# V for three of eight attention units, fetched as all-head tiles into the weight staging tiles

## The chip, the core and the metric

The kernel runs on one core of a Trainium2 chip. The number that counts is the device time of one execution in microseconds (us). Three runs of the kernel before took 2112.99, 2114.51 and 2115.87 us, so the median is 2114.51 us. The core has five engines that each work through an instruction list of their own: TensorE (PE, with its weight loads as PEld), VectorE (DVE), ScalarE (ACT), GpSimd (POOL) and SyncE (SP). SP issues all of this kernel's transfers between memory and the core.

## What is computed

A banded attention, and then a mixture of experts (MoE) whose routing weights are balanced by Sinkhorn iterations:

```python
scores = q @ k.T / sqrt(64) + bias          # 4 batches, 8 heads, 768 positions, 64 per head
a = softmax(scores where key < 8 or 0 <= pos - key < 96)
x = (a @ v) as (3072, 512)
P = exp(x @ w_gate - max)                   # (3072, 8)
for _ in range(8):
    P /= P.sum(1) + 1e-9; P /= P.sum(0) + 1e-9; P *= 3072 / 8
out = sum_e P[:, e] * (relu(x @ w1[e]) @ w2[e])
```

The expert products are made with fewer multiplications than the plain rule needs: sums and differences of blocks of x (named b11, b21, b22, t1 to t4) meet sums and differences of blocks of w1 (s1 to s4, a11, a12, a22), after Strassen. Each operand is split into a high and a low half, so a product is three matmuls.

## The kernel before, in words

**The attention.** It is worked in 8 units `u` of 384 rows (half a batch, all heads), each in 4 steps, one for a pair of heads. So there are 32 pairs n = 0 to 31, and unit u holds pairs 4u to 4u + 3. The change's "units 4 to 6" are u = 3, 4 and 5. In step n, PE multiplies the weights of pair n - 1 with V (`values`, tile `o_ps`), turns the weights of pair n (`t_ps`), transposes Q and K of pair n + 3 (`prepare`, tile `tp`) and makes the scores of pair n + 2 (`s_ps`). POOL copies parts of the key tile `kk` for the prepared pair (L278 to L285); the scores of that pair, a step later, need them. Between the steps (`between`) PE does pieces of other work: the gate and the first expert slices of finished rows (`filler`).

**V.** A pair's V is loaded by `load_v`, called by `flush` two pairs ahead, into the tile that the pair two before used: even pairs into a part of `acc` (`early_raw`), odd ones into `raw2`. For odd u a pair takes 6 transfers (L211 to L213 for each head), for even u 4 (L209, L230, L231).

**The sums of x.** When 4 tiles of 128 rows are finished, `sums_of` makes t3, t2, t1 and t4 of them (`combine`, from L706). For all but the last half of the last batch a sum is 5 POOL instructions: `xres` (L706, the low parts), `xsum` (L713), high part (L714), `xsum` (L715), low part (L716). The last half is made with `hurry`: only `xres` (L706) on POOL, then on DVE `xsum` (L708) and its sum with `xres` (L709), ACT rounds it (L710) and DVE takes the low part (L711). The four hurried sums follow each other, because t2 needs t3 and t4 needs t2, and because `xres` has one buffer.

**The experts' weights.** `stage_group` loads a slice of w1 and w2 into the staging tiles `w1f` and `w2f`, and POOL makes four sums of w1 in `wsum` (L637, 128x256 each). `make_group` splits all into high and low halves (ACT L619, POOL L620; tiles `w1ops`, `w2ops`, `s2ops`) and makes four sums of w2 in `wsum2` (L637). `stage` has one buffer for each of these tiles. Group 0 is staged by a call at the last unit, `make(0)` follows the attention, and group g + 1 is made while group g is multiplied.

**What sets the order.** The program hands its instructions to a scheduler, which orders each engine's list beforehand by its own estimate of when each can start. On the chip an engine then takes its list in that order. So an instruction that depends on little (staging group 0, for example) stands far ahead of its place in the code, and a change of one dependence moves instructions everywhere. PE's list in the attention is fixed by the code (`InOrder`); POOL's, DVE's, ACT's and SP's are not.

**The switch.** After the attention, PE multiplies group 0 for the last batch (`layer1_fast`): products p1 and p2 into `bank_x`, p6 into `bank_y` (needs t2), p5 and p3 into `bank_z` (p5 needs t1), p7 and p4 into `bank_w` (p4 needs t4). The Sinkhorn iterations (`ngm_ps`, `c_ps` on PE, small DVE instructions) run among them.

Of the kernel before, what the change touches and what calls it, by code (L numbers as in the profile page):

```python
# [8 lines left out]
F32 = mybir.dt.float32  # L9
# [8 lines left out]
P = 128  # L18
BIG = 2.0 ** 100
MAX_LOCAL = 97  # L20
MAX_GLOBAL = 32
SINKHORN_ITERS = 8
EPS = 1e-9
UT = 3
# [8 lines left out]
WARM2 = 2  # L33
AHEAD = 6
CHUNK = 3
LAG = 7
FG = 2
OPS = ("s1", "s2", "s3", "s4", "a11", "a12", "a22")
# [54 lines left out]
class InOrder:  # L93


    def __init__(self, tc):
        self.tc, self.engine = tc, tc.nc.tensor
# [8 lines left out]
class Banded:  # L106
# [6 lines left out]
    def __init__(self, tc, q, k, v, early):  # L113

        self.tc, self.nc = tc, tc.nc
        self.q, self.k, self.v = q, k, v
        self.H, self.D = q.shape[1], q.shape[3]
        H, nb = self.H, 3 * self.H * P
        self.bias1 = early[:, 0:2 * H * P].rearrange("p (h c) -> p h c", h=H)
        self.bias0 = early[:, 2 * H * P:nb].rearrange("p (h c) -> p h c", h=H)  # L120
        self.early_raw = early[:, nb:nb + self.RAW]
        nb += self.RAW
        self.d1 = early[:, nb:nb + 2 * P]
        self.d0 = early[:, nb + 2 * P:nb + 3 * P]
        self.gates = early[:, nb:nb + BU]
        self.work = [(b, half, g) for b in range(q.shape[0]) for half in range(2) for g in range(H // 2)]
        self.pending, self.waiting = [], []
        self.sums, self.inv, self.outs = {}, {}, {}
        self.pe = InOrder(tc)
        nb += 4 * P  # L130
        self.early_pT = [early[:, n:n + 4 * P].rearrange("p (c k) -> p c k", c=4) for n in (nb, nb + 4 * P)]
        assert nb + 8 * P <= early.shape[1]
        self.warm = early[:, -256:].bitcast(mybir.dt.bfloat16)
        self.qk, self.vs, self.ready, self.scored, self.far, self.copied, self.loaded = {}, {}, {}, {}, {}, {}, {}

    def open(self, ctx, ident, idle):
# [105 lines left out]
        self.qk[n] = q_r, k_r  # L242

    def load_v(self, n):
        if n >= len(self.work):
            return
        self.vs[n] = self.raw_tile(n, 2, 2)
        self.load_pair(self.vs[n], self.v, n)

    def prepare(self, t):  # L250

# [114 lines left out]
    def turn(self, t):  # L366
# [4 lines left out]
        for c, (u, a, _, _, _) in enumerate(blocks):  # L371
            self.pe.transpose(out=t_ps[:, c], in_=p_sb[:, u, a], identity=self.ident)
        pT = self.wrk.tile([P, 4, P], F32, name="pT", bufs=1) if t % CHUNK == 0 else self.early_pT[t % CHUNK - 1]
        copy = self.nc.vector.tensor_copy if self.idle and t % CHUNK == CHUNK - 1 else self.nc.scalar.copy
        copy(out=pT[:, 0:len(blocks)], in_=t_ps[:, 0:len(blocks)])
        return pT

    def values(self, n, group, pT, o_ps):

        D, v_r = self.D, self.vs[n]  # L380
        for c, (u, a, j, i, slots) in sorted(enumerate(self.blocks(n, group)), key=lambda b: b[1][1]):
            self.pe.matmul(o_ps[j * D:(j + 1) * D, i], lhsT=v_r[:, slots[a], j * D:(j + 1) * D],
                           rhs=pT[:, c], start=(a == 0), stop=(a == len(slots) - 1))

    def ahead(self, ts, warm=0):
# [6 lines left out]
    def unit(self, u, x, between):  # L392

        NG, per = len(GROUPS), len(GROUPS) * (self.H // 2)
        if u == 0:
# [7 lines left out]
            self.keep_warm(self.po, "o", WARM0)  # L403
            self.ahead(range(0, CHUNK - 1))
            self.scale_bias(2)
# [4 lines left out]
            self.keep_warm(self.po, "o", WARM1)  # L410
            self.ahead(range(CHUNK - 1, CHUNK))
            self.keep_warm(self.po, "o", WARM1)
            for t in range(CHUNK, AHEAD, CHUNK):
                self.ahead(range(t, t + CHUNK), WARM2)
            for t in range(2 * NG, AHEAD + NG):
# [28 lines left out]
    def flush(self):  # L444


        ended = None
        for n, group, pT, o_ps, g, x in self.pending:
            self.values(n, group, pT, o_ps)
            if group == len(GROUPS) - 1:  # L450
                ended = n, o_ps, g, x
        self.pending = []
        if ended is None:
            return
        n, o_ps, g, x = ended
        self.load_v(n + 2)
        self.nc.vector.tensor_tensor(out=o_ps, in0=o_ps, in1=self.inv.pop(n), op=ALU.mult)
        of = o_ps.rearrange("p t c -> p (t c)")
        for xh, xl, src, dst, width in x:
            self.nc.scalar.copy(out=xh[:, g, dst:dst + width], in_=of[:, src:src + width])  # L460
        for xh, xl, src, dst, width in x:
            self.nc.vector.tensor_tensor(out=xl[:, g, dst:dst + width], in0=of[:, src:src + width],
                                         in1=xh[:, g, dst:dst + width], op=ALU.subtract)
# [457 lines left out]
def pipeline(tc, attention, ident, moe, acc):  # L921
# [11 lines left out]
    with ExitStack() as top:  # L933
# [10 lines left out]
        stage = early.enter_context(tc.tile_pool(name="stage", bufs=1))  # L944
# [5 lines left out]
        pieces = att.enter_context(tc.tile_pool(name="pieces", bufs=4))  # L950
        fps = att.enter_context(tc.tile_pool(name="fps", bufs=2, space=PSUM))
        attention.open(att, ident, (fps, "fl"))
        xs, ops = {}, {}
        ws, spills, making = [], [], []

# [94 lines left out]
        slots = attention.SLOTS  # L1050
        bounds = [0]
        while bounds[-1] < TT - HB:
            t = bounds[-1]
            b = t // BT
            last = ((b + 1) * BT if (b + 1) * BT - t <= HB else t + (UT if b == 0 else HB))
            bounds.append(last)
        chunks = [(t // BT, t % BT, n - t) for t, n in zip(bounds, bounds[1:])]
        opens = [((n - 1) // UT + 1) * slots + LAG for n in bounds[1:]]
        closes = opens[1:] + [NU * slots]
# [12 lines left out]
        def between(n=1):  # L1072
            spill(n)
            now[0] += n
            if now[0] > slots and making:
# [3 lines left out]
                making.clear()  # L1079
            while halves and now[0] >= halves[0][0] * slots + LAG:  # L1080
                h = halves.pop(0)[1]
# [6 lines left out]
        for u in range(NU):  # L1088
            if (u + 1) * UT > (NB - 1) * BT and NB - 1 not in xs:
                while halves and halves[0][1] < 2 * (NB - 2):  # L1090
                    h = halves.pop(0)[1]
# [19 lines left out]
        while halves:  # L1111
            h = halves.pop(0)[1]
# [15 lines left out]
        b = NB - 1  # L1128
# [153 lines left out]
        for q, b in enumerate(order):  # L1282
            x_ops, x_next = x_next, {}
            ms = {}
            for g in range(NG):
# [4 lines left out]
                if g < PLAIN:  # L1290
                    h = Fast(moe, pbc[q, e], h32, spool2, hop)
# [78 lines left out]
def kernel(  # L1370
# [33 lines left out]
    with tc.If(rv > 0) as cmp:  # L1404
        pipeline(tc, band, ident, moe, acc)
    with cmp.Else():
        pipeline(tc, Dense(tc, q, k, v, ng, nl), ident, moe, acc)
# [32 lines left out]
```

## Time and profile before

| | us |
|---|---|
| median of 3 runs | 2114.51 |
| the profiled execution: its span, first to last instruction | 2114.1 |
| PE busy | 2089.4 (99%) |
| DVE busy | 1493.1 (71%) |
| POOL busy | 1511.4 (71%) |
| ACT busy | 742.2 (35%) |

The profiled execution has no time of its own beside its span; the median of the runs is 0.4 us longer than that span, well inside the 2.9 us between the fastest and the slowest run. Times in the rows are microseconds from the span's start. The attention lasts until about 261 us, the switch until about 300 us, and the rest is experts' products.

### The profile page before, as it was taken

The numbers are of one execution on the slowest core, as the hardware profiler recorded it, in microseconds if no ns is written. First come the engines' busy times: TensorE is split into PE (matmuls) and PEld (weight loads), VectorE is DVE, ScalarE is ACT, GpSimd is POOL, SyncE is SP. The second block draws the span as 40 slices with busy tenths as digits, with TensorE's granted clock in tenths as the row PEclk, the third lists the DMA queues.
The fourth block names the chain that finished last, engine by engine and source line by source line (L and its number), as shares of the span: only waits on it lengthen the run. The fifth ranks groups of instructions, "written<-read, shape, count | busy, mean of one in ns | idle before, by whom it ended". The sixth has DMA issues, their size and how long they took to land.

```text
span 2114.1 us, 31113 instructions
## 1 busy us (share of the span) xinstructions
PE 2089.4 (99%) x10435; PEld 1726.2 (82%) x10436; DVE 1493.1 (71%) x2280; ACT 742.2 (35%) x1535; POOL 1511.4 (71%) x1353
## 2 busy tenths in 40 slices
PE   8999999999999999999999999999999999999998
PEld 6887878888888888888888888888788888888887
DVE  7676599565555655557777777777667777777776
ACT  7888743332323333242222222222232222222221
POOL 5677897777767777357777777777677777777776
PEclk9999999999999999999999999999999999999999
DMA  6777566666565665697767766776976776667662
GB/s 147 187 203 197 154 248 243 235 230 246 219 251 214 234 239 218 249 379 204 204 194 203 203 196 201 204 203 195 362 221 196 201 204 203 195 204 204 193 194 83
DMA packets 294871, 452.39 MB, mean 214 GB/s; under 512 B 114160, under 2 KB 153264, under 8 KB 284336
## 3 DMA queue, kind: packets, MB, share of 16 engines
q1 hardware_dynamic: 294704, 450.31, 67.4%
q8 instruction: 87, 1.43, 0.3%
q14 instruction: 80, 0.66, 0.1%
HBM read 310.92 MB, written 139.30 MB: 213 GB/s over the span
## 4 chain that ended last, share of the span: by engine, by line
PE 92%; DVE 3%; ACT 2%; DMA 1%; issue 0%; POOL 0%; SPq 0%; ACTq 0%; DVEq 0%
PE m_ps L100 27%; PE y_ps L100 16%; PE bank_w L100 11%; PE bank_z L100 11%; PE bank_x L100 11%; PE bank_y L100 6%; PE o_ps L100 1%; PE t_ps L103 1%; PE s_ps L100 1%; PE h_ps L100 1%; DVE p_sb L338 1%; PE tp L103 1%; ACT p_sb L352 1%; PE y_ps L798 1%; PE y_ps L799 1%; PE y_ps L800 1%
## 5 line engine op out<-in xcount | busy, mean ns | idle before, releaser
L100 PE MATMUL m_ps<-hop,w2r 128*128 128x512 f32 x2520 | 639.5, 389 | 1.6 <-DVE m L1344 1.4
L1344 DVE TENSOR_TENSOR m<-m_ps,m 128x1024 f32<-128x1024 f32 x406 | 495.4, 1221 | 194.4 <-PE m_ps L100 191.2
L100 PEld LDWEIGHTS m_ps<-hop,w2r 128*128 128x128 f32 x2520 | 472.8, 188 | 100.6 <-DVE m L1344 1.8
L896 POOL TENSOR_TENSOR hop<-h,hop 128x512 fp32r<-128x512 f32 x180 | 234.3, 1301 | 302.8 <-ACT hop L895 302.8
L100 PE MATMUL y_ps<-w2ops,hop 128*128 128x512 f32 x1344 | 336.7, 389 | 0.1
L896 POOL TENSOR_TENSOR hop<-hsum,hop 128x512 fp32r<-128x512 f32 x240 | 306.7, 1300 | 0.9 <-ACT hop L895 0.9
L895 ACT CAST hop<-hsum 128x512 fp32r<-128x512 f32 x240 | 149.4, 623 | 427.0 <-POOL hsum L901 422.8
L100 PEld LDWEIGHTS y_ps<-w2ops,hop 128*128 128x128 f32 x1344 | 252.2, 188 | 52.9 <-DVE acc L1188 0.5
L1188 DVE SCALAR_TENSOR_TENSOR acc<-y_ps,pm,acc 128x512 f32<-128x512 f32 x240 | 179.8, 750 | 143.2 <-PE y_ps L100 141.4
L895 ACT CAST hop<-h 128x512 fp32r<-128x512 f32 x180 | 111.9, 621 | 378.6 <-DVE h L907 367.6
L100 PE MATMUL bank_w<-xr,w1r 128*128 128x512 f32 x744 | 189.0, 389 | 0.0
L100 PE MATMUL bank_z<-xr,w1r 128*128 128x512 f32 x744 | 189.0, 389 | 0.0
L100 PE MATMUL bank_x<-xr,w1r 128*128 128x512 f32 x744 | 188.9, 389 | 0.0
L901 POOL TENSOR_TENSOR hsum<-h,h 128x512 f32<-128x512 f32 x120 | 153.1, 1298 | 41.2 <-DVE h L907 41.1
L100 PEld LDWEIGHTS bank_x<-xr,w1r 128*128 128x128 f32 x744 | 139.6, 188 | 29.0
L100 PEld LDWEIGHTS bank_w<-xr,w1r 128*128 128x128 f32 x744 | 139.5, 188 | 28.9
L100 PEld LDWEIGHTS bank_z<-xr,w1r 128*128 128x128 f32 x744 | 139.5, 188 | 28.9
L901 POOL TENSOR_TENSOR hsum<-h,hsum 128x512 f32<-128x512 f32 x120 | 155.8, 1298 | 0.0
L637 POOL TENSOR_TENSOR wsum<-w1f 128x256 f32<-128x256 f32 x62 | 45.4, 753 | 92.7 <-DMA w1f<-in_moe_w_dram 92.5
L352 ACT ACTIVATE p_sb<-p_sb,mx 128x256 f32<-128x256 f32 (+1 forms) x192 | 93.3, 494 | 7.5 <-DVE mx L338 6.8
L100 PE MATMUL bank_y<-xr,w1r 128*128 128x512 f32 x372 | 94.4, 389 | 0.0
L772 DVE TENSOR_TENSOR t<-bank_y,t 128x512 f32<-128x512 f32 x93 | 64.2, 690 | 40.0 <-PE bank_y L100 39.3
(251 smaller groups left out, 3358.6 us busy)
## 6 DMA issues: line engine op xcount, KB each, us to landing
w1r<-w1s SPq DMA_DIRECT2D x434, 256.0 KB, 2.9
w2r<-w2s SPq DMA_DIRECT2D x420, 256.0 KB, 2.9
w1s<-w1ops SPq DMA_DIRECT2D x31, 1792.0 KB, 6.8
w2s<-s2ops SPq DMA_DIRECT2D x30, 1024.0 KB, 8.5
w2s<-w2ops SPq DMA_DIRECT2D x30, 768.0 KB, 7.7
w1f<-in_moe_w_dram SPq DMA_DIRECT2D x32, 512.0 KB, 7.9
w2f<-in_moe_w_dram SPq DMA_DIRECT2D x32, 512.0 KB, 8.4
xs_t<-piece SPq DMA_DIRECT2D x16, 512.0 KB, 3.5
```

What stands on the lines that cost most here:

```text
L100: return self.tc.keep_in_program_order(self.engine.matmul(*args, **kw))
L103: return self.tc.keep_in_program_order(self.engine.transpose(*args, **kw))
L338: nc.vector.tensor_tensor_reduce(out=pv, in0=s_list[u], in1=bias, scale=-(D ** -0.5), scalar=3.0e38, op0=ALU.add, op1=ALU.min, accum_out=m ...
L352: nc.scalar.activation(out=pv, in_=pv, func=AF.Exp, bias=mx[:, u:u + 1], scale=-1.0, accum_out=sm[:, i, j:j + 1])
L637: self.nc.gpsimd.tensor_tensor(out=s[:, n], in0=x, in1=y, op=op)
L772: tt(out=t, in0=bank["y"], in1=t, op=ALU.add)
L798: self.pe.matmul(y_ps, lhsT=hh, rhs=lf, start=(f == 0), stop=False, skip_group_check=True)
L895: self.nc.scalar.copy(out=t[:, 0], in_=full)
L896: self.nc.gpsimd.tensor_tensor(out=t[:, 1], in0=full, in1=t[:, 0], op=ALU.subtract)
L901: self.nc.gpsimd.tensor_tensor(out=t, in0=self.full[x], in1=self.full[y], op=ALU.subtract)
L1188: nc.vector.scalar_tensor_tensor(out=a, in0=y_ps, scalar=moe.pm[:, tt, e:e + 1], in1=a, op0=ALU.mult, op1=ALU.add)
L1344: nc.vector.tensor_tensor(out=ms[p], in0=bank, in1=ms[p], op=ALU.add)
```

## The change

For u = 3, 4 and 5 (`WIDE`) V is loaded for all four pairs at once, as tiles of 128 keys by 8 heads by 64 (512 columns), while the unit before is worked (`load_wide`, called by `flush` for the pair four ahead). `load_v` skips these units. The tiles are the staging tiles: halves of `w1f`, `w2f` and `wsum` for u = 3 and 5, halves of `wsum2` and one half each of `early_raw` and `raw2` for u = 4. `values` takes each block of V from a list in place of one tile. The 64 transfers of V for these units (24, 16 and 24) become 23 (9, 5 and 9) with the same bytes.

```diff
+WIDE = (3, 4, 5)
...
     def load_v(self, n):
-        if n >= len(self.work):
+        if n >= len(self.work) or n // self.pairs in self.wide:
             return
...
+    def wide_tiles(self, u):
+        stage, W = self.stage, self.H * self.D
+        if u % 2:
+            ts = [stage.tile([P, 4, 2 * P], F32, name="w1f"), stage.tile([P, 2, 4 * P], F32, name="w2f"),
+                  stage.tile([P, 4, 2, P], F32, name="wsum")]
+            flat = [t.rearrange("p a c -> p (a c)") for t in ts[0:2]] + [ts[2].rearrange("p a b c -> p (a b c)")]
+            return [t[:, n * W:(n + 1) * W] for t in flat for n in range(2)]
+        pair = stage.tile([P, 4, 2 * P], F32, name="wsum2").rearrange("p a c -> p (a c)")
+        return [pair[:, 0:W], pair[:, W:2 * W], self.early_raw[:, 2 * UT * P:2 * UT * P + W],
+                self.raw.tile([P, 2 * UT * P], F32, name="raw2")[:, 0:W]]
+
+    def load_wide(self, n):
+        u, part = divmod(n, self.pairs)
+        if u not in self.wide or part == self.pairs - 1:
+            return
...
+        ts, G, dma = self.wide[u], MAX_GLOBAL, self.nc.sync.dma_start
+        own = ts[1 + part] if half == 0 else ts[2 * part + 1]
+        dma(out=own, in_=rows[:, half * UT + part])
+        if half == 1:
+            dma(out=ts[2 * part][G:], in_=rows[G:, UT - 1 + part])
+            dma(out=ts[2 * part][0:G], in_=rows[0:G, 0])
+        elif part == 0:
+            dma(out=ts[0][0:G], in_=rows[0:G, 0])
+            dma(out=ts[0][G:], in_=rows[G:, 1])
...
-            self.pe.matmul(o_ps[j * D:(j + 1) * D, i], lhsT=v_r[:, slots[a], j * D:(j + 1) * D],
+            self.pe.matmul(o_ps[j * D:(j + 1) * D, i], lhsT=v_r[slots[a]][:, j * D:(j + 1) * D],
...
         self.load_v(n + 2)
+        self.load_wide(n + self.pairs)
```

Since `w1f`, `w2f` and `wsum` hold V until u = 5 has read it, the staging of expert group 0 comes after that. In POOL's list the eight sums of group 0 move from the third unit to the seventh (u = 6), and this moves what stands behind them. Line numbers of the changed kernel are larger by 39 or 40 from `prepare` on.

POOL's list where u = 6 begins, before (`xsum` and `xres` are the first instructions of a sum of x, `kk` and `far` the key copies of pair 27):

```order
L713 TENSOR_TENSOR xsum<-xh 128x512
L706 TENSOR_TENSOR xres<-xl 128x512
L278 COPY kk<-kk 128x2x32
L279 COPY kk<-kk 128x2x96
L278 COPY far_3672<-kk 128x2x32
L279 COPY far_3672<-kk 128x2x96
L283 COPY kk<-far_3298 128x2x128
```

and of the change, the same place:

```order
L753 TENSOR_TENSOR xsum<-xh 128x512
L677 TENSOR_TENSOR wsum<-w1f 128x256 x2
L746 TENSOR_TENSOR xres<-xl 128x512
L677 TENSOR_TENSOR wsum<-wsum,w1f 128x256
L317 COPY kk<-kk 128x2x32
L318 COPY kk<-kk 128x2x96
L317 COPY far_3633<-kk 128x2x32
L318 COPY far_3633<-kk 128x2x96
L677 TENSOR_TENSOR wsum_4632<-w2f 128x256 x2
L322 COPY kk<-far_3266 128x2x128
```

Three of the sums of w1 of group 0 now stand ahead of the key copies, and the first of them reads `w1f`, which is fetched only when u = 5 has read its V from it.

POOL's list at the switch, before (the `xres` are those of the four hurried sums t3, t2, t1 and t4; the first `w1ops` and `w2ops` are the splits of group 0, the `wsum` are of group 1):

```order
L620 TENSOR_TENSOR w1ops<-w1f,w1ops 128x2x256
L706 TENSOR_TENSOR xres<-xl 128x512
L620 TENSOR_TENSOR w1ops<-wsum,w1ops 128x4x256
L620 TENSOR_TENSOR w1ops<-w1f,w1ops 128x256
L620 TENSOR_TENSOR w2ops<-w2f,w2ops 128x2x256 x2
L706 TENSOR_TENSOR xres<-xl 128x512 x2
L637 TENSOR_TENSOR wsum<-w1f 128x256 x2
L706 TENSOR_TENSOR xres<-xl,xh 128x512
```

and of the change, from the first hurried `xres` to the third (all others are of group 1; `wsum_4796` is `wsum2`):

```order
L746 TENSOR_TENSOR xres<-xl 128x512
L677 TENSOR_TENSOR wsum<-w1f 128x256 x2
L677 TENSOR_TENSOR wsum<-wsum,w1f 128x256
L660 TENSOR_TENSOR w1ops<-w1f,w1ops 128x2x256
L660 TENSOR_TENSOR w1ops<-w1f,w1ops 128x256
L677 TENSOR_TENSOR wsum<-w1f,wsum 128x256
L746 TENSOR_TENSOR xres<-xl 128x512
L677 TENSOR_TENSOR wsum_4796<-w2f 128x256 x2
L660 TENSOR_TENSOR w2ops<-w2f,w2ops 128x2x256 x2
L660 TENSOR_TENSOR w1ops<-wsum,w1ops 128x4x256
L677 TENSOR_TENSOR wsum_4796<-wsum_4796,w2f 128x256
L746 TENSOR_TENSOR xres<-xl 128x512
```

The splits of group 0 now all stand ahead of the first `xres`, 6 instructions of group 1 stand between the first and the second, and 6 more between the second and the third.

PE's list at the same switch, of the change (`y_ps` is the last filler work, `bank_y` needs t2 and `bank_z` needs t1):

```order
L851 MATMUL y_ps<-w2h,fhop 128x512
L890 MATMUL ngm_ps<-gmax,ones 128x1
L901 MATMUL c_ps<-pm,ones 128x192
L770 MATMUL bank_y<-xh,w1ops 128x512
L771 MATMUL bank_y<-xh,w1ops 128x512
L772 MATMUL bank_y<-xh,w1ops 128x512
L770 MATMUL bank_y<-xh,w1ops 128x512
L771 MATMUL bank_y<-xh,w1ops 128x512
L772 MATMUL bank_y<-xh,w1ops 128x512
L901 MATMUL c_ps<-pm,ones 128x192 x2
L770 MATMUL bank_z<-xh,w1ops 128x512
```

Before, the one `ngm_ps` stood between `bank_y` and `bank_z` and the first `c_ps` came later; the matmuls of `y_ps`, `bank_y` and `bank_z` follow each other in the same order in both.

## Rows read from the trace of the kernel before

**Rows 1.** The page: busy time by engine, and the chain that ended last.

```profile
PE 2089.4 (99%) x10435; PEld 1726.2 (82%) x10436; DVE 1493.1 (71%) x2280; ACT 742.2 (35%) x1535; POOL 1511.4 (71%) x1353
...
PE 92%; DVE 3%; ACT 2%; DMA 1%; issue 0%; POOL 0%; SPq 0%; ACTq 0%; DVEq 0%
```

**Rows 2.** Windows (us from:to; length, busy and count by engine, clock, DMA).

```profile
320.00:340.00 20.00, 20.00 (x91) 16.60 (x89) 19.13 (x37) 6.63 (x11) 14.27 (x13) 1.00 0.72 277
```

**Rows 3.** Waits of PE, 0 to 500 us (waiter <- releaser: us in total, times, longest).

```profile
PE o_ps L100 <- DMA raw<-in_v_dram: 2.6, 3, 1.3
...
PE tp L103 <- DMA raw<-in_q_dram: 1.2, 1, 1.2
...
PE o_ps L100 <- DMA acc<-in_v_dram: 0.6, 1, 0.6
```

**Rows 4.** Timeline of PE (start, us, instruction, [idle before <- releaser]).

```profile
158.84 0.43 PE L100 MATMUL o_ps<-pT,raw 128*64 128x128 f32 x2 [1.25 <-DMA raw<-in_v_dram]
...
277.45 0.39 PE L730 MATMUL bank_y<-xh,w1ops 128*128 128x512 f32 x1
...
281.00 0.50 PE L730 MATMUL bank_z<-xh,w1ops 128*128 128x512 f32 x1 [1.71 <-DVE xh L711]
```

**Rows 5.** Instructions on V's tensor: ns min/median/max, first and last start.

```profile
L211 SPq DMA_DIRECT2D acc<-in_v_dram x16: 382/418/907, 39.1 to 235.5; - x16
```

**Rows 6.** Timeline of POOL, u = 6 to the switch.

```profile
230.20 0.50 POOL L285 CAST kk<-kk 128x384 fp32r<-128x384 f32 x1 [1.72 <-DVE kk L270]
...
235.88 1.27 POOL L714 TENSOR_TENSOR xl<-xsum,xres 128x512 fp32r<-128x512 f32 x1
...
242.46 2.37 POOL L620 TENSOR_TENSOR s2ops<-wsum,s2ops 128x1024 fp32r<-128x1024 f32 x1
...
257.94 1.28 POOL L714 TENSOR_TENSOR xl<-xsum,xres 128x512 fp32r<-128x512 f32 x1
...
262.11 1.75 POOL L620 TENSOR_TENSOR w1ops<-w1f,w1ops 128x512 fp32r<-128x512 f32 x1 [0.16 <-ACT w1ops L619]
...
271.50 1.28 POOL L706 TENSOR_TENSOR xres<-xl 128x512 f32<-128x512 f32 x1
274.73 1.29 POOL L706 TENSOR_TENSOR xres<-xl 128x512 f32<-128x512 f32 x1 [1.95 <-DVE xsum L709]
276.92 2.25 POOL L637 TENSOR_TENSOR wsum<-w1f 128x256 f32<-128x256 f32 x2 [0.89 <-DMA w1f<-in_moe_w_dram]
...
281.50 2.97 POOL L620 TENSOR_TENSOR w1ops<-w1f,w1ops 128x512 fp32r<-128x512 f32 x2
284.43 0.73 POOL L637 TENSOR_TENSOR wsum<-w1f,wsum 128x256 f32<-128x256 f32 x1
285.12 2.05 POOL L637 TENSOR_TENSOR wsum<-w2f 128x256 f32<-128x256 f32 x2
287.14 2.55 POOL L620 TENSOR_TENSOR w2ops<-w2f,w2ops 128x512 fp32r<-128x512 f32 x2
```

**Rows 7.** Timeline of ACT, u = 7.

```profile
240.40 1.05 ACT L619 CAST s2ops<-wsum 128x1024 fp32r<-128x1024 f32 x1
...
242.35 0.56 ACT L826 COPY acc<-g_ps 16x512 f32<-16x512 f32 x1
```

**Rows 8.** Timeline of DVE at the switch.

```profile
265.14 2.87 DVE L709 TENSOR_TENSOR xsum<-xsum,xres 128x512 f32<-128x512 f32 x1 [2.44 <-POOL xres L706]
...
277.89 0.67 DVE L709 TENSOR_TENSOR xsum<-xsum,xres 128x512 f32<-128x512 f32 x1
...
279.70 1.25 DVE L711 TENSOR_TENSOR xh<-xsum,xh 128x512 fp32r<-128x512 f32 x1
```

**Rows 9.** Instructions on w1f: its transfers from issue to landing.

```profile
DMA to landing us min/median/max: 3.5/7.9/9.2
```

**Rows 10.** Windows at the end of the span (columns as Rows 2).

```profile
2108.00:2110.00 2.00, 0.35 (x4) 0.11 (x2) 1.40 (x2) 0.00 (x0) 0.00 (x0) 1.00 0.38 140
2110.00:2112.00 2.00, 0.00 (x0) 0.00 (x0) 0.00 (x0) 0.00 (x0) 0.00 (x0) 0.58 0.40 146
```

More of the change, by code (lines that the diff above doesn't have):

```diff
@@ L133, in __init__ @@
         self.warm = early[:, -256:].bitcast(mybir.dt.bfloat16)
+        self.pairs = self.H // 2
+        self.wide = dict.fromkeys(WIDE)
         self.qk, self.vs, self.ready, self.scored, self.far, self.copied, self.loaded = {}, {}, {}, {}, {}, {}, {}
@@ L244, in load_v @@
     def load_v(self, n):
-        if n >= len(self.work):
+        if n >= len(self.work) or n // self.pairs in self.wide:
             return
-        self.vs[n] = self.raw_tile(n, 2, 2)
-        self.load_pair(self.vs[n], self.v, n)
+        t = self.raw_tile(n, 2, 2)
+        self.load_pair(t, self.v, n)
+        self.vs[n] = [t[:, s] for s in range(2 * UT)]
+    def wide_tiles(self, u):
[12 more added lines that the diff above has]
+            return
+        b, half, _ = self.work[n]
+        rows = self.v[b].rearrange("h (t p) d -> p t h d", p=P)
+        if part == 0:
+            ts = self.wide_tiles(u)
+            for m in range(self.pairs):
+                cols = slice(m * P, (m + 1) * P)
+                self.vs[u * self.pairs + m] = [t[:, cols] for t in ts]
+            self.wide[u] = [t.rearrange("p (h d) -> p h d", d=self.D) for t in ts]
+        ts, G, dma = self.wide[u], MAX_GLOBAL, self.nc.sync.dma_start
[7 more added lines that the diff above has]
+            dma(out=ts[0][G:], in_=rows[G:, 1])
     def prepare(self, t):
@@ L952, in pipeline @@
         attention.open(att, ident, (fps, "fl"))
+        attention.stage = stage
         xs, ops = {}, {}
```

## The prediction

> **What bounds the kernel now.** I read the page first, then the windows, PE's waits, and the timelines of PE, POOL and DVE around the places that the change touches.
>
> PE is busy for 2089.4 of 2114.1 us and stands for 92% of the chain that ended last [rows 1]. After the switch it never idles: in 320 to 340 us it is busy 20.00 of 20 us at a granted clock of 1.00 [rows 2]. So a delay of PE before 300 us shifts everything behind it and is never won back, and a stall removed there is won in full. Two places matter: what PE waits for in the attention, and when it gets through the switch.
>
> In the attention the waits for loads are 2.6 us on V in `raw` (three times, the longest 1.3 us; the one at 158.84 stands in the rows), 0.6 us on V in `acc` and 1.2 us on Q [rows 3, 4]. All lie in u = 4 and 5, which are among the changed units.
>
> At the switch PE has one real wait: `bank_z` at 281.00 waits 1.71 us for the DVE instruction that writes t1 [rows 4]. Behind it stands a chain of POOL: the last key copy of the attention at 230.20, then sums and splits with hardly a pause until the `xres` of t1 at 274.73 [rows 6]. It takes 50.8 us from 230.20 to 281.00. The change alters POOL's list here.
>
> **The change, part by part.**
>
> *Waits on loads.* With V there a unit ahead, the V waits go: 2.6 + 0.6 = 3.2 us. The wait on Q goes too if fewer transfers stand before Q's on SP: 1.2 us. I take the whole, g = 4.4 us; the least is 0, if the other loads become late in their turn.
>
> *Transfers.* They become 41 fewer, which costs nothing. But the first of u = 3 are now issued at about 13 us, between loads that the start needs. Six of them at 0.418 us of SP each [rows 5] are 2.5 us. The start has other work in DVE and ACT that covers this; I take 0, at most 1 us without that cover.
>
> *Staging of group 0 in u = 6.* The eight sums of w1, 0.73 us each (at 284.43) [rows 6], are 5.8 us of POOL, and three of them now stand ahead of the key copies of pair 27. POOL has pauses there, so I take 0; a rival below has the other end. What these sums displace, though, comes later: behind the copy of pair 31 POOL now has 8 instructions of sums of x, where 4 stood between that copy and 235.88.
>
> *The switch.* I add up POOL's new list, with the durations of the old one, from the key copy of pair 31, whose time PE sets. It comes g earlier: 230.20 − 4.4 = 225.8.
>
> - the copy, 0.5: 226.3
> - 8 instructions of sums at 1.3 (the one at 235.88) [rows 6]: 236.7. Before, 4 of them took the 5.2 us up to 235.88.
> - one more sum to 238.0, then `s2ops` must wait for ACT's half. ACT's cast (1.05 us) follows a copy that ended at 242.91 [rows 7], so 242.91 + 1.05 − 4.4 = 239.6: a wait of 1.6.
> - the same instructions as from 235.88 to 257.94, 22.06 us: 236.7 + 1.6 + 22.1 = 260.4
> - the last sum of the first half and all splits of group 0, now ahead of every hurried `xres`: 271.50 − 257.94 less one `xres` of 1.28 that stood among them, 12.3: 272.7. This is the work that the list of before interleaved with the first `xres`.
> - the first `xres` (t3), 1.28: 274.0
> - six instructions of group 1: 2.25 + 0.73 + 2.97 + 0.73 (276.92 to 284.43) [rows 6] = 6.7: 280.7
> - the second `xres` (t2), 1.28: 281.9. Now `bank_y` can follow; before it began at 277.45 [rows 4].
> - six more: 2.05 + 2.55 + 2.37 + 0.73 = 7.7 (at 285.12, 287.14, 242.46 and 284.43) [rows 6]: 289.6
> - the third `xres` (t1), 1.29: 290.9
> - from there to `bank_z`, before: 274.73 + 1.29 = 276.02 to 281.00, 5.0 us. In that stretch DVE did other things. The bare links are its sum (0.67), ACT's rounding and the low part (1.25) [rows 8]. The rounding fits into the 1.1 us between those two, so I take 0.6 for it: 2.5.
>
> So `bank_z` comes at 290.9 + 5.0 = 295.9 at the latest by this sum. At the earliest, POOL runs uncontended. Pairs of `wsum` at 2 × 0.73 in place of 2.25 and 2.05 save 1.4. Splits at the rate of the `s2ops` row (2.37 us for 1024 elements, so 6.5 for the 2816 of group 0) save 1.6 against the 8.1 us they took (262.11 to 271.50 less one `xres`). That gives 290.9 − 3.0 + 2.5 = 290.4. Against 281.00 the shift of all that follows is +9.4 to +14.9 us. g is already in it, since the chain starts with it. I take +11, nearer the low end: PE and DVE will mostly be waiting there, so little work stands in the way of a sum that has become ready.
>
> *Why DVE matters here.* The DVE sum at 265.14 took 2.87 us and the same instruction at 277.89 took 0.67 [rows 8]; during the first POOL ran splits, during the second it ran a pair of `wsum`. [...] The row at 277.89 speaks against a loss every time.
>
> *The clock.* PE idles before `bank_y`: its work up to there ends at 277.45 − 4.4 = 273.1, and t2 comes at about 282 to 285. Then it idles again before `bank_z`. [...] I take 2, in the lower part, since only what follows `bank_z` counts. [...] That the clock falls without work, [rows 10] agree; how it rises again no run here shows.
>
> *Sum.* 2114.1 + 11 + 2 = 2127 us. The profiled execution is 0.4 us below the median of the runs, too little to correct for. A difference under 0.2% (4.2 us) can't be told from no change; 13 us is 0.6%.
>
> **Rivals.**
>
> 1. *The loads' stalls go and POOL takes its added work into its pauses.* Then `bank_z` comes 4.4 us earlier: 2109.7 us, faster. For it speaks that POOL is busy only 71% of the span [rows 1]. Against it: from 230.20 to the switch its rows follow each other with few pauses, and 0.89 and 1.95 us are the long ones [rows 6]. It decides if the stretch of 50.8 us to `bank_z` grows by less than 4.4 us; the added instructions alone are 5.2 + 6.7 + 7.7 = 19.6 us. If it grows by about that, the time is the same.
>
> [...]
>
> 3. *`w1f` lands late.* Its transfers can be issued only when `values` of pair 23 has read V from it, and took 3.5 to 9.2 us to landing, in the middle 7.9 [rows 9]. The `wsum` that reads it stands ahead of the key copies of pair 27, and PE's scores of that pair wait for those. At 3.5 us POOL is only just in time; at 7.9 PE loses some 2.5 us in u = 6 (an estimate: 4.4 us later, less about 2 of slack). Everything behind moves by that, so 2129.5 us.
>
> 4. *The change doesn't do what it says:* V is there, but Q or K, which SP now issues behind eight wide transfers, are late in their place. g goes to 0 or below and everything starts 4.4 later: 2131.4 us.
>
> **How the numbers follow.** Main line 0.50 (2127, its own range 2122 to 2131), clock at its bound 0.12, `w1f` late 0.15, Q and K late 0.08, faster by rival 1 0.10, its middle case of no change 0.05. The range of 2116 to 2134 leaves out rival 1 and a little above. Faster 0.10, same 0.05, slower 0.85.
>
> **What the profile of the changed kernel would show.** Right: no wait of `o_ps` on V in u = 4 and 5; PE waits of several us at `bank_y` and `bank_z`, both put down to the DVE writes of the hurried sums; on POOL the three first hurried `xres` at about 273, 281 and 290, with two blocks of group 1 of 6 to 8 us between them; a granted clock below 1.00 right after `bank_y`; from about 300 us on the same busy rows, 9 to 15 us later. The prediction would be wrong in its core if the three `xres` came within 5 us of each other, or if `bank_z` began before 281. It would be wrong in the upstream part if PE waited for `in_q` or `in_k` in u = 4 and 5 for more than before, or if the key copy of pair 31 were not about 4 us earlier.

## The result and the profile after

The changed kernel takes 2130.86 us (median of 5 runs, 2130.0 to 2131.87), the kernel before 2114.76 us. The ratio is 1.0075 with a 95% interval of 1.0064 to 1.0085: slower by 16 us. The forecast was 2127, its range 2116 to 2134.

The page's busy line of the changed kernel. The work is the same as in [rows 1]; PE's 3 us more are a net: at the switch its matmuls are busy 6.5 us longer, at a clock of 0.65 in the mean, and elsewhere 3.4 us shorter.

```profile
PE 2092.5 (98%) x10435; PEld 1729.1 (81%) x10436; DVE 1487.4 (70%) x2280; ACT 742.2 (35%) x1535; POOL 1510.2 (71%) x1353
```

PE's waits of the changed kernel from 256 us to the end, where before the longest was the 1.7 us at `bank_z`:

```profile
PE c_ps L901 <- DVE pm L898: 10.6, 2, 5.7
PE bank_y L770 <- DVE xh L751: 7.3, 1, 7.3
```

PE's waits in the attention, the only one left on V (compare [rows 3]). It lies at 46.37 us, ahead of the units with wide V:

```profile
PE o_ps L101 <- DMA acc<-in_v_dram: 0.3, 1, 0.3
```

To see what the attention gave and what the switch took, I split the span at the last filler matmul before `bank_y`. What lies ahead of it I call the head, the rest the tail. PE's timeline of before at that place, and of the changed kernel through the switch:

```profile
277.22 0.40 PE L811 MATMUL y_ps<-w2h,fhop 128*128 128x512 f32 x1
```

```profile
270.08 0.39 PE L851 MATMUL y_ps<-w2h,fhop 128*128 128x512 f32 x1
...
276.50 1.01 PE L901 MATMUL c_ps<-pm,ones 128*128 128x192 f32 x2 [5.73 <-DVE pm L898]
284.85 0.79 PE L770 MATMUL bank_y<-xh,w1ops 128*128 128x512 f32 x1 [7.34 <-DVE xh L751]
...
293.31 0.98 PE L901 MATMUL c_ps<-pm,ones 128*128 128x192 f32 x2 [4.82 <-DVE pm L898]
294.35 0.80 PE L770 MATMUL bank_z<-xh,w1ops 128*128 128x512 f32 x1
294.94 0.63 PE L771 MATMUL bank_z<-xh,w1ops 128*128 128x512 f32 x1
...
299.42 0.39 PE L770 MATMUL bank_x<-xl,w1ops 128*128 128x512 f32 x1
```

The head is 277.22 − 270.08 = 7.1 us shorter. The tail is 2130.1 − 270.08 = 1860.0 us, against 2114.1 − 277.22 = 1836.9, so 23.1 us longer. From the last filler to `bank_z` PE needs 24.3 us in place of 281.00 − 277.22 = 3.8 [rows 4]: that is 20.5 of the 23.1. Another 2.7 come behind `bank_z`.

POOL of the changed kernel, the answers to [rows 6]: the key copies of pair 31, and the three first hurried `xres`.

```profile
223.96 0.50 POOL L324 CAST kk<-kk 128x384 fp32r<-128x384 f32 x1 [3.06 <-DVE kk L309]
...
236.70 2.36 POOL L660 TENSOR_TENSOR s2ops<-wsum,s2ops 128x1024 fp32r<-128x1024 f32 x1 [0.54 <-ACT s2ops L659]
...
268.04 1.28 POOL L746 TENSOR_TENSOR xres<-xl 128x512 f32<-128x512 f32 x1
270.21 1.85 POOL L677 TENSOR_TENSOR wsum<-w1f 128x256 f32<-128x256 f32 x2 [0.88 <-DMA w1f<-in_moe_w_dram]
...
276.20 1.38 POOL L746 TENSOR_TENSOR xres<-xl 128x512 f32<-128x512 f32 x1
...
281.80 2.45 POOL L660 TENSOR_TENSOR w1ops<-wsum,w1ops 128x1024 fp32r<-128x1024 f32 x1
284.21 1.17 POOL L677 TENSOR_TENSOR wsum<-wsum,w2f 128x256 f32<-128x256 f32 x1
285.34 1.80 POOL L746 TENSOR_TENSOR xres<-xl 128x512 f32<-128x512 f32 x1
```

The `xres` stand 8.2 and 9.1 us apart, with the two blocks of group 1 between. DVE of the changed kernel from behind the second `xres` to `bank_z` (compare [rows 8]):

```profile
279.42 1.23 DVE L906 TENSOR_SCALAR csum<-csum 128x8 f32<-128x8 f32 x1
280.68 1.37 DVE L907 TENSOR_TENSOR pm<-pm,csum 128x192 f32<-128x192 f32 x1
...
282.35 2.44 DVE L751 TENSOR_TENSOR xh<-xsum,xh 128x512 fp32r<-128x512 f32 x1
...
285.33 0.68 DVE L748 TENSOR_TENSOR xsum<-xh 128x512 f32<-128x512 f32 x1
285.93 0.29 DVE L897 RECIPROCAL rsum<-rsum 128x24 f32<-128x24 f32 x1
286.25 1.10 DVE L898 TENSOR_TENSOR pm<-pm,rsum 128x192 f32<-128x192 f32 x1
287.82 0.69 DVE L812 TENSOR_TENSOR t<-bank_y,t 128x512 f32<-128x512 f32 x1 [0.46 <-PE bank_y L772]
288.52 0.36 DVE L903 TENSOR_REDUCE csum<-c_ps 128x8 f32<-128x192 f32 x1
...
289.61 0.41 DVE L906 TENSOR_SCALAR csum<-csum 128x8 f32<-128x8 f32 x1
290.05 0.36 DVE L907 TENSOR_TENSOR pm<-pm,csum 128x192 f32<-128x192 f32 x1
...
290.92 0.69 DVE L749 TENSOR_TENSOR xsum<-xsum,xres 128x512 f32<-128x512 f32 x1
291.52 0.30 DVE L897 RECIPROCAL rsum<-rsum 128x24 f32<-128x24 f32 x1
291.85 1.31 DVE L898 TENSOR_TENSOR pm<-pm,rsum 128x192 f32<-128x192 f32 x1
293.08 1.21 DVE L751 TENSOR_TENSOR xh<-xsum,xh 128x512 fp32r<-128x512 f32 x1
```

`xres` of t1 is done at 287.14, but its sum (L749) begins at 290.92. In DVE's list a Sinkhorn step stands between, which reads `c_ps`, which PE makes behind `bank_y`, which waited for t2. So one late sum delays the next through PE. PE's clock there, from the windows (columns as Rows 2):

```profile
272.00:276.00 4.00, 0.00 (x0) 0.00 (x0) 3.47 (x6) 1.92 (x4) 4.00 (x5) 0.90 0.16 62
276.00:280.00 4.00, 1.01 (x2) 0.50 (x2) 2.83 (x6) 1.52 (x2) 4.00 (x5) 0.50 0.42 131
...
296.00:300.00 4.00, 4.00 (x12) 3.12 (x12) 3.86 (x8) 0.62 (x1) 3.84 (x5) 0.61 0.63 262
300.00:304.00 4.00, 4.00 (x20) 3.11 (x18) 3.89 (x10) 1.07 (x2) 0.39 (x1) 1.00 0.00 0
```

### The profile page after: what moved, and what is told of

It reads as the page before. It is cut to its first block, busy times and chain, and to the rows that moved or that the text cites. A ratio compares the mean times of both kernels' runs of the same rounds, so it can differ in the third digit from the quotient of the medians.

```text
span 2130.1 us, 31024 instructions
## 1 busy us (share of the span) xinstructions
PE 2092.5 (98%) x10435; PEld 1729.1 (81%) x10436; DVE 1487.4 (70%) x2280; ACT 742.2 (35%) x1535; POOL 1510.2 (71%) x1353
## 4 chain that ended last, share of the span: by engine, by line
PE 94%; DVE 3%; ACT 1%; DMA 1%; issue 0%; POOL 0%; SPq 0%; ACTq 0%; DVEq 0%; POOLq 0%
PE m_ps L101 27%; PE y_ps L101 16%; PE bank_x L101 11%; PE bank_z L101 11%; PE bank_w L101 11%; PE bank_y L101 6%; PE o_ps L101 2%; PE t_ps L104 1%; PE s_ps L101 1%; PE h_ps L101 1%; PE tp L104 1%; PE y_ps L839 0%; PE y_ps L838 0%; PE y_ps L840 0%; PE g_ps L101 0%; PE r_ps L104 0%
```

## The experiments

Head and tail by the split above, in us against the profile of before (so the last filler less 277.22, and the span less that filler less 1836.9). The head of one kernel varies by itself: V by pairs gives 0.0, +1.6 and −2.8 in three profiles, wide V with unchanged staging −7.1, −6.8, −5.7 and −8.0. The tail is what the edits at the switch change. Medians of runs lie between 0.3 us below and 4 us above the span of the profile.

| kernel | last filler | span | head | tail | median |
|---|---|---|---|---|---|
| before | 277.22 | 2114.1 | 0 | 0 | 2114.8 |
| changed | 270.08 | 2130.1 | −7.1 | +23.1 | 2130.9 |
| late staging alone | 278.86 | 2117.1 | +1.6 | +1.3 | 2118.2 |
| list of the change alone | 274.38 | 2134.0 | −2.8 | +22.7 | 2136.8 |
| changed, group 1 behind | 270.38 | 2121.9 | −6.8 | +14.6 | 2125.7 |
| changed, Sinkhorn behind | 271.53 | 2133.9 | −5.7 | +25.5 | 2136.3 |
| changed, both behind | 269.27 | 2118.3 | −8.0 | +12.1 | 2121.3 |
| changed, sums on DVE | 272.81 | 2115.9 | −4.4 | +6.2 | 2119.9 |
| the same, Sinkhorn behind | 274.33 | 2114.6 | −2.9 | +3.4 | 2116.4 |
| the same, DVE's sums later | 273.44 | 2113.6 | −3.8 | +3.3 | 2113.3 |
| the same, p7 first | 271.29 | 2112.0 | −5.9 | +3.8 | 2113.7 |
| the same, ten more matmuls | 271.24 | 2113.8 | −6.0 | +5.7 | 2115.6 |
| wide V in u = 4 alone | 276.21 | 2130.5 | −1.0 | +17.4 | 2132.3 |

**1. The late staging alone**, in the kernel before:

```diff
-                with attention.behind(12):
+                with attention.behind(26):
                     staged = moe.stage_group(*groups[0], stage)
```

> The kernel before with one edit: the staging of expert group 0 is held back until the key copies of pair 26, where the change has it; V is loaded by pairs as before. Theory (the loss is made at the switch, by POOL's list there: group 1 stands between the hurried xres): that list stays nearly as before here, two wsum of group 1 before the last xres only, so 0 to 3 us above before, 2115 to 2118 us, with no PE wait at bank_y and a bank_z wait below 5 us. Rival 1 (the late staging by itself makes POOL late by the 5.8 us of its eight sums): bank_z 5 to 6 us later, 2120 us or more. Rival 2 (the wide transfers or the tiles do it): no change, 2114 to 2115 us.

Measured: 2118.17 us, ratio 1.0012 (1.0003 to 1.0021). PE's row at the switch is that of before, with the same wait:

```profile
282.65 0.50 PE L730 MATMUL bank_z<-xh,w1ops 128*128 128x512 f32 x1 [1.71 <-DVE xh L711]
```

The edit holds back the four sums of w1 only (193.6 to 198.3 us); the four of w2 stay at 69 to 72 us, where the change has all eight at 193 to 205. So late sums of w1 are not what made the 16 us, as rival 1 would have it. The tail is 1.3 us longer, and the whole 2.7 us against the runs of before beside it, at the upper edge of the theory's 0 to 3.

**2. Group 1 behind the hurried sums**, in the changed kernel:

```diff
-        nc.gpsimd.tensor_tensor(out=r, in0=x[1], in1=y[1], op=op)
+        self.res = nc.gpsimd.tensor_tensor(out=r, in0=x[1], in1=y[1], op=op)
...
-                if n == 1:
+                if n == 1 and g == 0:
+                    with tc.issue_after(moe.res.ins):
+                        make(make_next)
+                elif n == 1:
                     make(make_next)
```

> The changed kernel with one edit: POOL's work of group 1 is held back until the last of the four hurried xres. Theory: first xres still at about 268, the next two as soon as DVE has used the one before, about 271.5 and 275, t1 2.5 to 5 us after the end of the third, so bank_z at 279 to 281 in place of 294.4, no clock below 1.00 behind it, and 2112 to 2116 us. Rival 1 (the late staging decides, not the order at the switch): 2120 to 2126 us. Rival 2 (PE's and DVE's lists decide, the Sinkhorn iterations that stand ahead of t1's sum): the xres come early but DVE's sums don't, bank_z at 288 or later, 2122 us or more.

Measured: 2125.66 us, ratio 1.0047 (1.0033 to 1.0061): 5 us won, where 15 to 19 were expected. PE at the switch:

```profile
276.71 1.01 PE L901 MATMUL c_ps<-pm,ones 128*128 128x192 f32 x2 [5.62 <-DVE pm L898]
...
278.38 0.79 PE L770 MATMUL bank_y<-xh,w1ops 128*128 128x512 f32 x1 [0.67 <-DVE xh L751]
...
283.42 0.80 PE L770 MATMUL bank_z<-xh,w1ops 128*128 128x512 f32 x1 [2.12 <-DVE xh L751]
```

`bank_z` comes 11 us earlier than in the change. But PE still waits for `c_ps` ahead of `bank_y`, the clock is 0.50 in 276 to 284, and 5.4 us are lost behind `bank_z`. More than half of that is waits that the kernel before doesn't have, 0.7 us at 360.66 and this one:

```profile
363.58 0.50 PE L101 MATMUL bank_x<-xl,w1ops 128*128 128x512 f32 x1 [2.66 <-ACT t L810]
```

The theory was too simple: POOL's list is a part, PE's and DVE's Sinkhorn places are another, as rival 2 had it.

**3. Sinkhorn behind the hurried sums, with POOL's list of the change, and 4. both together:**

```diff
-            if n % 6 == 5:
+            if n % 6 == 5 and n < 11:
                 next(sinkhorn, None)
+            elif n % 6 == 5:
+                with tc.issue_after(moe.lows[-3 if n == 11 else -2].ins):
+                    next(sinkhorn, None)
```

`moe.lows` holds DVE's instructions for the low parts of the hurried sums: `lows[-3]` is that of t2, `lows[-2]` that of t1.

> The changed kernel with one edit on the Sinkhorn iterations: DVE takes their first maximum over all rows only behind t2's low part, and the first iteration behind t1's. POOL's list at the switch stays that of the change (12 instructions of group 1 between the first and third xres). Theory (POOL's list and the Sinkhorn work ahead of the sums each hold up PE): xres as in the change, the third at 285, then t1 without the Sinkhorn work in between, bank_z at 290 to 291 in place of 294.4, the clock still low behind it, 2125 to 2127 us. Rival A (POOL's list alone matters): no change from 2131. Rival B (the Sinkhorn work alone matters): bank_z near 281, 2115 to 2117 us.

Measured: 2136.28 us, ratio 1.0098 (1.0083 to 1.0114). A clear miss: slower than the change itself, against all three expectations. The wait for `c_ps` turned into one of 10.5 us at `bank_y`, t1 came 2 us earlier only, and 8.7 us were lost behind `bank_z` in place of 2.7. A likely reading, not shown: while POOL makes t2 late, the Sinkhorn steps fill a wait that is there anyway, and held back they come later for nothing.

> The changed kernel with both edits: POOL's work of group 1 behind the last hurried xres, and the Sinkhorn work behind the hurried sums. Theory: bank_y at about 276, bank_z at 278 to 279; PE has still idled 5 us before bank_y, so the clock is low and costs some 2.5 us, and the late group 1 costs 2 to 3 us after 360: 2116 to 2120 us, against 2125.7 with the first edit alone. Rival A (Sinkhorn work is harmless): 2124 to 2126 us. Rival C (the clock costs nothing): 2113 to 2116 us.

Measured: 2121.33 us, ratio 1.0029 (1.0018 to 1.0041), 4.3 us below group 1 behind alone, a little above what the theory gave. With POOL's list mended, the Sinkhorn place is worth something. PE still waits 7.2 us for t2, since POOL reaches the first `xres` at 267.30 only, 2.0 us ahead of PE's last filler; before it was at 263.82, 13.4 us ahead. The splits of group 0 still stand in front of it.

**5. The sums of w1 of group 0 on DVE**, in the changed kernel:

```diff
-            self.nc.gpsimd.tensor_tensor(out=s[:, n], in0=x, in1=y, op=op)
+            (on or self.nc.gpsimd).tensor_tensor(out=s[:, n], in0=x, in1=y, op=op)
...
-                    staged = moe.stage_group(*groups[0], stage)
+                    staged = moe.stage_group(*groups[0], stage, nc.vector)
```

> The changed kernel with one edit: the four sums of w1 of group 0 are made by DVE in place of POOL. Nothing orders POOL's list at the switch by hand, but it comes out nearly as that of before, with two wsum of group 1 ahead of the last xres only. Theory: POOL needs the 50.8 us of before from the key copy of pair 31 to bank_z, and that copy comes 6 us earlier, so bank_z at about 275, no low clock, 2108 to 2110 us. Rival 1 (late staging): POOL still has the sums of w2 late, 2 to 3 us of it, 2117 us. Rival 2 (the wide transfers cost somewhere else): 2114 us or more.

Measured: 2119.87 us, ratio 1.0021 (1.0012 to 1.003), 11 us below the change but not the 2108 to 2110 expected. `bank_z` began at 279.85 and not at about 275. Of the 6.2 us by which the tail is longer than before, 3.3 lie ahead of `bank_z`, with a wait of 2.2 us at `c_ps`, and 2.9 behind it. A new loss lies in the attention, where DVE stands idle for 3.0 us up to its first sum of `w1f`, with `qq` queued behind it. A row of PE in this run:

```profile
194.23 0.50 PE L101 MATMUL y_ps<-w2l,fhop 128*128 128x512 f32 x1 [3.18 <-DVE qq L309]
```

**6. The same with the Sinkhorn work behind, and 7. with DVE's sums held until the key low part of pair 28:**

> The changed kernel with the sums of w1 of group 0 on DVE and the Sinkhorn work behind the hurried sums. PE's list at the switch is then that of before (bank_y, ngm_ps, bank_z, no c_ps between). Theory: t2 and t1 as in the run with DVE alone, bank_y at 274, bank_z at 276 to 277 in place of 279.9, and the clock stays at 1.00, since PE has no wait above 2 us: 3 us for bank_z and 3 us for the clock less, span 2109 to 2111 us, median 2110 to 2114 us. Rival A (Sinkhorn work is harmless): 2119 to 2121 us.

Measured: 2116.43 us, ratio 1.0005 (0.9996 to 1.0014), 3.4 us below run 5 and 2.4 above the theory's 2110 to 2114: PE's last filler came 1.5 us later than in run 5, `bank_z` at 279.98 as there and not at 276 to 277, after a wait of 2.2 us, and the clock did not stay at 1.00 throughout (0.61 in 280 to 284).

```diff
-                with attention.behind(12):
+                with attention.behind(12), attention.behind_low(28):
```

> As the run before this one, with DVE's sums of w1 held behind the key low part of pair 28, so that DVE doesn't stand waiting for w1f while PE needs qq. Theory: the PE wait of 3.2 us on qq at 194 goes; the sums are needed only at 257, so nothing is late: 2 to 3 us faster than the run before, span 2106 to 2109 us, median 2107 to 2112 us, below the kernel before. Rival D (what is won in the attention is lost again at the switch, where POOL's sums set t1): the same time as the run before.

Measured: 2113.26 us, ratio 0.9988 (0.9979 to 0.9997): 3.2 us less, and the wait on `qq` is down to 0.3 us, but 1.3 us above the theory's 2107 to 2112. The two profiles differ by 1.0 us only, so that the 3.2 are that wait is not shown. This version is faster than both kernels, than the one before by 0.12%, just clear of the noise.

**8. The switch's list alone**, in the kernel before (V by pairs, group 0 staged early):

```diff
-                s = staged if g == 0 else moe.stage_group(*groups[g], stage)
+                s = staged if g == 0 else fetched if g == 1 else moe.stage_group(*groups[g], stage)
...
             if n == FG * KT - 1:
+                fetched = moe.stage_group(*groups[1], stage)
-                with tc.issue_after(moe.low.ins):
+                with tc.issue_after(moe.low.ins), tc.issue_after(moe.summed.ins):
                     for _ in last_sums:
```

> The kernel before, V by pairs and group 0 staged early, with one edit: group 1's slices are fetched and its four sums of w1 made ahead of t2's xres. The lists at the switch then come out as those of the change: six instructions of group 1 between the first and second xres, six between the second and third, ngm_ps and c_ps ahead of bank_y. Theory (the order of the lists at the switch alone makes the loss): block 1 starts when w1f has landed, about 277, so the second xres at 284, the third at 292 to 293, bank_z at 297 to 300, low clock behind it, 2132 to 2138 us. Rival (wide V or the late staging is needed for the loss): 2114 to 2118 us.

Measured: 2136.76 us, ratio 1.0101 (1.0085 to 1.0116), inside the theory's range. POOL and PE of this run:

```profile
274.14 1.41 POOL L637 TENSOR_TENSOR wsum<-w1f 128x256 f32<-128x256 f32 x2 [5.44 <-DMA w1f<-in_moe_w_dram]
...
279.05 1.28 POOL L706 TENSOR_TENSOR xres<-xl 128x512 f32<-128x512 f32 x1
...
288.29 1.72 POOL L706 TENSOR_TENSOR xres<-xl 128x512 f32<-128x512 f32 x1
```

```profile
PE c_ps L861 <- DVE pm L858: 13.7, 4, 4.8
PE bank_y L730 <- DVE xh L711: 3.4, 1, 3.4
```

The tail grows by 22.7 us, almost the change's 23.1, without any wide V. So a list of this kind at the switch is enough for a loss of that size. That the two numbers are so close is in part chance. Here POOL reaches the first `xres` early (260.98), then waits 5.4 us for `w1f` where the change waits 0.9, and one more Sinkhorn step stands ahead of `bank_z`. The theory's time came true by other steps as well: the second and third `xres` came 4 to 5 us earlier than it says, and `bank_z`, at 298.90, 8.9 us behind the end of the third.

**9. p7 ahead of p5, and 10. ten matmuls to keep PE busy**, both on run 7's version:

```diff
+            if p == "p5" and self.swap:
+                bank["w"] = ps.tile([P, BU], F32, name="bank_w", tag="h")
+                self.products(bank["w"], w["s3"], x["t3"], True, False)
...
```

The product made here is p7; its own place behind is then passed over.

> The version with wide V, the sums of w1 of group 0 on DVE, the Sinkhorn work held back and DVE's sums held behind the key low part of pair 28, with one more edit: at the switch PE makes p7 (bank_w, needs only t3) ahead of p5 (bank_z, needs t1). Theory: p7's six matmuls, 1.4 us, fill the wait for t1, of which 1 us is left; the clock stays at 1.00, so bank_z's matmuls cost 0.23 us each and not 0.43: 2 to 3 us faster than without the edit, span 2110 to 2112 us, median 2110 to 2113 us. Rival (the clock falls all the same, or t4 comes late): 2113 us, as without it.

```diff
+        self.idle = {"p5": 10}
...
+            for _ in range(self.idle.pop(p, 0)):
+                self.pe.matmul(bank[o], lhsT=x["t2"][0][:, 0, 0:P], rhs=x["t2"][0][:, 0], start=True, stop=True, skip_group_check=True)
```

The product p5 behind these ten overwrites what they made.

> The same version without the reordering in the code, and with ten matmuls of t2 into bank_z whose result is overwritten, between bank_y and t1 (the scheduler moves p7 ahead of p5 too). Theory: PE has no pause over 1 us, the clock stays at 1.00, but the ten matmuls take 2.2 us, so bank_z starts at 280.3 and the gain is 1 to 2 us against the version without, median 2111 to 2113 us. Rival (the low clock costs nothing): 1 us slower than the version without, 2114 to 2115 us.

Measured: 2113.70 us (0.9991, 0.9982 to 1.0) and 2115.58 us (1.0001, 0.9992 to 1.001): no gain, and a loss of about the ten matmuls' 2.2 us. The rivals were right. The windows of run 7 and then of run 9 show that run 9 kept the clock, and what bounds instead:

```profile
276.00:280.00 4.00, 1.70 (x7) 1.17 (x6) 3.88 (x7) 2.10 (x4) 3.37 (x3) 0.87 0.26 100
280.00:284.00 4.00, 4.00 (x14) 3.11 (x14) 4.00 (x7) 0.62 (x1) 4.00 (x5) 0.70 0.00 0
```

```profile
276.00:280.00 4.00, 3.09 (x13) 2.18 (x13) 4.00 (x6) 1.67 (x4) 4.00 (x4) 1.00 0.00 0
280.00:284.00 4.00, 2.95 (x14) 2.50 (x14) 4.00 (x7) 1.52 (x3) 4.00 (x5) 1.00 0.00 0
```

DVE (third pair) is busy 4.00 of 4 us in both kernels in 280 to 284. With the clock at 1.00 PE only waits for DVE: 1.05 us at the second `bank_z` of run 9.

**11. Wide V in u = 4 alone** (`WIDE = (4,)`). In this run, by its code, loads by pairs overwrite part of the V of u = 4, so some of its values come from other data.

> The changed kernel with WIDE = (4,): only u = 4 has wide V, in wsum2 and two tiles of the attention, so the staging of group 0 is not late. POOL's list at the switch has all splits of group 0 ahead of the first xres and five instructions of group 1 ahead of t1's (the third). Theory: PE gains 2 to 3 us upstream, but t1 is late: bank_z at 285 to 287, 2118 to 2121 us. Rival 1 (late staging decides): the gain alone, 2111 to 2112 us. Rival 2 (the wide transfers cost): 2115 us or more with a PE wait on a load upstream.

Measured: 2132.34 us, ratio 1.0082 (1.0069 to 1.0096). Neither `w1f` nor `wsum` holds V here, and the sums of w1 of group 0 are early (83 to 89 us), yet the switch's list changes (t1's `xres` behind five instructions of group 1) and the tail grows by 17.4 us. The sums of w2, though, come at 164 to 173 us, against 69 to 72 before: they go into `wsum2`, which holds V of u = 4. The direction is the theory's; its 2118 to 2121 was 11 us too low: `bank_z` came at 290.89 and not by 287, behind waits of 4.6 us at `bank_y` and 5.8 at `bank_z`, and 6.5 us more went behind it.

## Why the prediction was right, and where it was off

The time lies in the range, and the way it was lost is in the main the one forecast: the load stalls go, POOL's hurried `xres` move apart, PE waits ahead of `bank_y` and `bank_z`, the clock falls (0.50 in 276 to 280). One sign came otherwise: of PE's 17.9 us of waits at the switch 7.3 are at `bank_y`, none is at `bank_z` itself, and 10.6 are at the `c_ps` in front of both.

That the number came near is in part luck: POOL was done with the third `xres` 3.8 us earlier than the sum's 290.9, and the step behind it took 4.7 us more than its 2.5. The sum goes by spans. Against the span of 2130.1 it is 3.1 us short, 2.4 of them ahead of `bank_z` and 0.7 behind. (The profiled execution of the changed kernel took 2131.87 us, 1.8 more than its span; the 0.4 us that the prediction set aside compare two executions.) By the time alone rival 4, with 2131.4, lies nearer than the main line; the trace speaks against it, since the head became shorter. By steps:

- **Waits on loads.** The waits on V and Q in u = 4 and 5 went; 0.3 us on V at 46.37 and 0.7 us on K (0.4 before) are left. g was taken as 4.4; the head is 7.1 us shorter in this pair of profiles. Over the three profiles with V by pairs (mean −0.4) and the four with wide V (mean −6.9) it is 6.5. The size was short by 2, since one profile of a head that varies by 4.4 us can't give it. Of the 6.5, 3.0 are busy time of PE: up to the last filler it is busy 263.7 us in the mean of the three and 260.7 in that of the four, for the same number of matmuls. Why is open.
- **Staging in u = 6.** Taken as 0. The first `wsum` waits 2.6 us for `w1f`, up to 193.4, but PE waits for no key copy in u = 6 (its only wait for one, 0.7 us, lies at 27.65). So 0 was right; rival 3 named a wait that exists, on POOL, and PE paid nothing for it.
- **POOL's chain.** Forecast for the three `xres`: 272.7, 280.7, 289.6. Measured: 268.04, 276.20, 285.34. The steps between (8.0 and 8.9 forecast) are 8.2 and 9.1. The start is 1.8 us earlier through the copy of pair 31, and the stretch from there to the first `xres` 44.1 us and not 46.9, mainly since the splits took 7.0 us and not 8.1 and ACT was waited for 0.54 us and not 1.6.
- **From t1's `xres` to `bank_z`: the step that failed.** Taken as 2.5, at most 5.0, with the reason that DVE would mostly be waiting. It is 294.35 − 287.14 = 7.2 us. DVE's list had Sinkhorn work ahead of the sum, which hangs on PE's `c_ps` behind `bank_y`. The lists printed ahead of the prediction show `c_ps` in front of `bank_y`, and the prediction gave it no price. Run 4 against run 2, and run 6 against run 5, show that it has one (4.3 and 3.4 us for Sinkhorn alone) once POOL is out of the way. This error of 4.7 us met the chain's 3.8 the other way, so `bank_z` was late by 13.4 us and not 11.
- **DVE beside POOL.** t2's sum (at 278.45) took 1.04 us and t1's 0.69, against 0.67 in [rows 8]: 0.4 us together. t2's low part, though, took 2.44 us, against 1.25 in [rows 8], beside POOL's split at 281.80. The two Sinkhorn steps in front of it (L906 and L907) took 1.23 and 1.37 us, against 0.41 and 0.36 for the same steps at 289.61 and 290.05. Together that is 3.0 us ahead of `bank_y`, through which t1's sum came late; that POOL is the cause is not shown.
- **The clock.** The 2 us in the sum were the author's estimate, and no run shows them; the trace of the changed kernel shows 2.3 in their place. From `bank_z` to the next product, 12 matmuls took 5.07 us, at a clock of 0.54 in 292 to 296 and 0.61 in 296 to 300; at 0.23 us, as from 299.42 on, they take 2.8. But runs 9 and 10 (a clock of 1.00 in 276 to 284, where run 7 had 0.87 and 0.70, and no gain) show that such a price can be hidden under DVE, so that the whole 2.3 stands on the path in the change is likely and not shown. From 300 on, with PE busy 4.00 us of the first 4, the clock was 1.00.

What was not seen: that the reordering doesn't hang on the tiles `w1f` and `wsum`. The text of the change laid it to the staging that comes later; runs 1 and 11 show that late sums of w1 leave the switch alone, and that wide V in u = 4, with these sums early, reorders it too. The sums of w2 remain a suspect: they are late in the change and in run 11, and early in run 1. But run 5 has them late as well (195 to 204 us), with a list near that of before, so they don't do it alone. What in the scheduler's estimates tips the order was not tried.

Behind `bank_z` runs 2, 3 and 4 lose 5.4, 8.7 and 4.8 us. Waits of PE that the kernel before doesn't have are 3.3, 4.8 and 1.9 of these, and the low clock right behind `bank_z` 1.6, 2.1 and 2.2. The rest is open.

## What to carry to other kernels

When a change touches a kernel whose lists a scheduler orders, compare the lists at the tightest place of the program, however far from the edit: here a gain of 6.5 us in the attention was paid back more than threefold at a switch whose code had not changed. Price every instruction that now stands ahead of a critical one on each engine, and follow what that one waits for in turn; a wait that passes through two engines' lists, as here from t2 through PE's `c_ps` to t1's sum, doesn't show in either list alone. And take a gain that rests on transfer waits from several profiles.

## What the runs showed of the hardware

PE waited 1.71 us at `bank_z` in the kernel before, and the clock stayed at 1.00; in run 9 it waited 1.1 us at `bank_y` and 0.9 at `bank_z`, and the clock stayed at 1.00 too. In run 7 it waited 2.3 us at `bank_z`, after 1.1 us at `bank_y`, and the clock was 0.87 in 276 to 280 and 0.70 in 280 to 284; in run 6, after 1.1 and 2.2 us, it was 1.00 and then 0.61. So at the switch pauses of 2.2 and 2.3 us came with a loss of clock. Run 2's wait of 2.66 us at 363.58 did not: the clock was 1.00 in 360 to 400. The table of waits alone doesn't show which.
